# Four output stores moved from SyncE's DMA queue to ScalarE's, in a fused attention and expert-mixture kernel

## The chip, the cores and the metric

The kernel runs on one NeuronCore of a Trainium2 chip. The metric is the device time in microseconds (us) of one execution; lower is better. A core has five engines, each with its own instruction stream that runs in order: TensorE (PE in the profile; its weight loads are PEld), VectorE (DVE), ScalarE (ACT), GpSimd (POOL) and SyncE (SP). They wait for each other by semaphores. DMAs are issued from SyncE, ScalarE and GpSimd.

## The reference

```python
def _attn_ref(q, k, v, is_retrieval, n_sink, window):
    ...
    scores = scale * np.matmul(q, k.transpose(0, 1, 3, 2))
    ...
    mask = np.where(retr[0, :, 0, 0, None, None], full_mask, stream_mask)
    scores = np.where(mask[None, :, :, :], scores, -1000000000.0)
    ...
    a = a / (np.sum(a, axis=-1, keepdims=True) + 1e-09)
    return np.matmul(a, v).astype(np.float32)

def _moe_ref(x, domain_probs, w1, w2):
    ...
    p = domain_probs / (domain_probs.sum(-1, keepdims=True) + 1e-09)
    ...
    for e in range(E):
        h = np.maximum(x @ w1[e], 0.0)
        out += p[:, e:e + 1] * (h @ w2[e])
    return out.astype(np.float32)
```

Attention has 4 batches, 8 heads, 768 positions and 64 values per head. Three heads ("retrieval") see all earlier positions; the other five ("streaming") see 4 sink positions and a window of 64. The output, 3072 tokens of 512 values, goes through 4 experts of 512 to 1024 to 512, whose results are added with the token's weights `p`.

## The kernel before

Tokens are worked on in 24 tiles of 128. Attention runs over 8 pieces (batch and half, 384 positions each); three token tiles come out of each piece, transposed, as `xT`. The experts follow behind, interleaved with later attention pieces: the Python code emits a few matmuls of the expert work, then as much of the next attention piece as a plan allows. That emission is the order in which each engine runs its instructions; nothing reorders it afterwards.

The expert work has two forms. The first four token tiles are computed plainly, by `plain_steps`: tiles 0 to 2 together, then tile 3 alone. For each expert, eight groups of matmuls (L950, each group into one of four rotating PSUM banks named `pA`) make the hidden layer, a relu on ScalarE (L963) writes it to SBUF, and the matmuls of L971 make the output rows in a bank `pO`. VectorE (L983, L987) scales them by the expert's weight and adds them up in an fp32 accumulator `acc[nt]`. After the last expert the accumulator is complete and goes to memory by one DMA of 128 rows of 2 KB (L992).

The other twenty tiles go in pairs, by `pair_steps`. L1062 makes the hidden layers, again through the four `pA` banks, a relu on ScalarE (L1071) writes them, and the products of L1095 follow.

Both forms share one large SBUF buffer, `hA`. The accumulators lie in parts of it that the pairs use as blocks of hidden values:

```python
    blocks = hA.rearrange("p (b k x) -> p b k x", b=6, k=KT)
    ...
    def acc_of(nt):
        n0 = 2 * FTP * CH + nt * 2 * DM if nt < 3 else 6 * KT * P - 2 * DM
        return hA[:, n0 : n0 + 2 * DM].bitcast(FP32)
```

By these offsets `acc[0]` and `acc[1]` lie in block 3, `acc[2]` in block 4 and `acc[3]` in block 5. The third relu of the first pair writes the start of block 3, so it has to wait until the store of `acc[0]` has read it.

SyncE's queue also carries, in order of emission: the weights of a pair spread over all partitions (`pB`, L1012), the transposes of the next attention piece's queries (`qT`, three of them, L268) and keys (`kR` for retrieval heads, `kS` for streaming heads, L255), the copies of the sink rows (L249, L250), transposes of attention outputs (`xT`, L701) and the stores of the pairs (L1123). GpSimd issues the loads from memory (`kRr`, `kSr`, `q`, `vR`, `vS`). Around the end of the plain tiles SyncE's order is: `xT`, `pB`, three `qT`, `kR`, sink row, sink copy, `kS`, the four stores, and then the sink copies and transposes for the following attention piece.

The four stores are emitted at four places: three as the tiles 0, 1 and 2 end, in the last expert's turn, and the fourth as tile 3 ends. On ScalarE the exponentials of attention (L645), the relus (L963, L1071) and the row factors of streaming heads (L757, L767) run in the order of emission.

Of the kernel before, what the change touches and what calls it, by code (L numbers as in the profile page):

```python
# [17 lines left out]
def kernel(  # L18
# [33 lines left out]
    nc = tc.nc  # L52
    P = 128
# [44 lines left out]
    def bank():  # L98
        return pA.tile([P, 512], FP32, name="pA", bufs=4)
# [263 lines left out]
    for h in range(H):  # L363
        if h == 2:
            nc.sync.dma_start(
                out=v_s32, in_=v[0, :, 0:NS, :].rearrange("h r d -> r h d")
# [16 lines left out]
        out=probs, in_=moe_domain_probs.rearrange("(t p) e -> p t e", p=P)  # L383
# [121 lines left out]
    def mm_ns(cols):  # L505
        return cols / 2.4 + 2.5
# [424 lines left out]
    acc = {}  # L931
# [5 lines that stand above are left out]
    def plain_steps(nt0, tiles, e, tokens, n0):  # L937

        cols_n = tiles * P
        hs = hA[:, n0 : n0 + FTP * cols_n].rearrange("p (f x) -> p f x", f=FTP)  # L940
        require(nt0 // 3)
        x = tokens()
        ahead = 4 if nt0 == 0 and e == 0 else 1
        for f0 in [0, *range(ahead, FTP)]:
            pss = {ft: bank() for ft in range(f0, f0 + (1 if f0 else ahead))}
            cts = (0, 2, 1, 3)

            def layer1(ft, n):
                ct = cts[n]
                nc.tensor.matmul(  # L950
                    out=pss[ft][:, 0:cols_n],
                    lhsT=w1sb[:, e * DMP + ct, ft * P : (ft + 1) * P],
                    rhs=x[:, ct, :],
                    start=(n == 0),
                    stop=(n == DMP - 1),
                )

            for ft in pss:
                for n in range(DMP - 1):
                    layer1(ft, n)  # L960
            for ft, ps in pss.items():
                layer1(ft, DMP - 1)
                nc.scalar.activation(  # L963
                    out=hs[:, ft, :], in_=ps[:, 0:cols_n], func=AF.Relu
                )
                yield DMP * mm_ns(cols_n), 0.6
        for j in range(tiles):
            nt = nt0 + j
            ps_o = pO.tile([P, DM], FP32, name="pO", bufs=2)
            for ft in range(FTP):  # L970
                nc.tensor.matmul(  # L971
                    out=ps_o,
                    lhsT=hs[:, ft, j * P : (j + 1) * P],
                    rhs=w2sb[:, e * FTP + ft, :],
                    start=(ft == 0),
                    stop=(ft == FTP - 1),
                )
                if ft == FTP // 2 - 1:
                    yield FTP // 2 * mm_ns(DM), 1.4
            p_ap = p_sb[:, nt, e : e + 1]  # L980
            if e == 0:
                acc[nt] = acc_of(nt)
                nc.vector.tensor_scalar(  # L983
                    out=acc[nt], in0=ps_o, scalar1=p_ap, scalar2=None, op0=ALU.mult
                )
            else:
                nc.vector.scalar_tensor_tensor(  # L987
                    out=acc[nt], in0=ps_o, scalar=p_ap, in1=acc[nt],
                    op0=ALU.mult, op1=ALU.add,
                )  # L990
            if e == E - 1:
                nc.sync.dma_start(out=out[nt * P : (nt + 1) * P, :], in_=acc[nt])  # L992
            yield FTP // 2 * mm_ns(DM), 1.4

    PT = 2
# [170 lines left out]
    def moe_steps():  # L1166
        for e in range(E):
            if e == 1:
                turn_probs()
            yield from plain_steps(0, 3, e, lambda: xT[0], (e % 2) * FTP * CH)  # L1170
            weight_sums(e)
        for e in range(E):
            n0 = 2 * FTP * CH + 3 * 2 * DM + (e % 2) * FTP * P
            yield from plain_steps(3, 1, e, lambda: xT[1][:, :, 0:P], n0)
            if e + 1 < E:
                last_weight_sum(e)
            if e == E - 3:
                scale_inputs(pairs[0], 0)
        for n, nt0 in enumerate(pairs):
            yield from pair_steps(nt0, pairs[n + 1] if n + 1 < len(pairs) else None)  # L1180
# [56 lines left out]
    def require(a):  # L1237
        drained = False
        while state["a"] <= a:
            attention_step()  # L1240
            drained = True
        if drained:
            tick(LAG)
# [48 lines left out]
```

## Time and profile before

| | us |
|---|---|
| median of 4 runs | 398.21 (397.71 to 400.85) |
| the profiled execution | 398.11 |
| its span, first to last instruction | 396.3 |
| PE busy in the span | 378.5 (96%) |
| ACT, DVE, POOL busy | 233.9, 219.3, 139.8 |
| stores of the plain tiles, from issue to landing | 7.1 (median of 4, 256 KB each) |
| stores of the pairs, from issue to landing | 2.7 (median, 256 KB each) |

The span is what the profile's times are measured in; the execution's own time has some 1.8 us more around it. An engine that is busy 96% of the span sets the time, so the question for any edit is whether that engine's idle time changes. A wait in the profile is put down to the event that ended it: "A <- B" is time that A's engine stood before A until B was done. A busy share is an average over stages, and the stage in which the edit lies, from 70 to 110 us, is read by itself.

### The profile page before, as it was taken

What the parts mean: (1) busy time and instruction counts of PE and PEld (TensorE: products, weight loads), DVE (VectorE), ACT (ScalarE), POOL (GpSimd) and SP (SyncE); (2) the same over time, 40 slices, a digit from 0 to 9 for tenths busy, and PEclk for the clock granted to TensorE, in tenths of its full rate; (3) what the DMA queues carried; (4) which work ended last, traced back from release to release, by engine and by line L of the source; (5) the groups of instructions that cost most, each with busy time, mean ns of one, the idle gap of its engine ahead of it and who ended that gap; (6) DMA issues with size and microseconds to landing.
All of it is one profiled execution on the core that took longest, in us unless ns stands there. A gap on an engine that the chain in (4) does not pass through costs nothing.

```text
span 396.3 us, 9358 instructions
## 1 busy us (share of the span) xinstructions
PE 378.5 (96%) x3814; PEld 314.2 (79%) x3814; DVE 219.3 (55%) x472; ACT 233.9 (59%) x476; POOL 139.8 (35%) x182
## 2 busy tenths in 40 slices
PE   7889999989599998999999999999999999999996
PEld 4655556657498887889988898889988898888885
DVE  7734787556166456565653556655644547454340
ACT  4743568645468777574774578574774568361640
POOL 8833655927407533660464004651300000000000
PEclk9989999999899999999999999999999999999999
DMA  8999999999999999999899936999790210110101
GB/s 163 158 206 196 182 186 173 149 107 151 204 146 139 158 154 96 140 170 165 103 152 126 129 95 51 142 205 135 96 178 2 69 55 12 55 53 2 55 0 55
DMA packets 167632, 47.67 MB, mean 120 GB/s; under 512 B 156493, under 2 KB 161317, under 8 KB 167589
## 3 DMA queue, kind: packets, MB, share of 16 engines
q0 software_dynamic: 102656, 20.98, 69.2%
q1 hardware_dynamic: 63332, 25.70, 35.4%
q8 instruction: 30, 0.49, 0.5%
q10 hardware_dynamic: 1600, 0.39, 0.5%
q14 instruction: 14, 0.11, 0.1%
HBM read 48.82 MB, written 6.34 MB: 139 GB/s over the span
## 4 chain that ended last, share of the span: by engine, by line
PE 69%; DMA 11%; issue 8%; POOL 7%; ACT 2%; DVE 1%; POOLq 0%; ACTq 0%
PE pA L1062 28%; PE pO L1095 24%; PE pA L950 5%; PE pO L971 4%; DMA vS<-in_v_dram 3%; PE pA L627 3%; DMA kR<-kRr 3%; POOL vS L281 2%; DMA q<-in_q_dram 2%; DMA vS<-sinks 2%; PE pV L675 1%; DMA kS<-kSr 1%; PE pV L739 1%; POOL vR L279 1%; ACT es L645 1%
## 5 line engine op out<-in xcount | busy, mean ns | idle before, releaser
L1062 PE MATMUL pA<-xs,w1sb 128*128 128x256 f16 x1280 | 148.4, 274 | 4.2 <-ACT hA L1071 4.2
L1062 PEld LDWEIGHTS <-w1sb 128*128 128x128 f16 x1280 | 124.2, 98 | 19.5 <-issue 4.4
L1071 ACT ACTIVATE hA<-pA 128x512 f16<-128x512 f32 x160 | 94.8, 597 | 46.7 <-PE pA L1062 38.2
L1095 PEld LDWEIGHTS <-hA 128*128 128x128 f16 x1120 | 105.7, 98 | 12.5
L645 ACT ACTIVATE es<-pA 128x384 f16<-128x384 f32 (+2 forms) x122 | 59.9, 511 | 33.6 <-PE pA L627 30.9
L1095 PE MATMUL pO<-w2sb,hA 128*128 128x256 f16 x640 | 79.0, 272 | 0.0
L1028 DVE TENSOR_TENSOR xs<-xT,pB 128x1024 f16<-128x1024 f16 (+1 forms) x52 | 49.6, 974 | 23.5 <-PE pA L1062 23.2
L1095 PE MATMUL pO<-tsb,hA 128*128 128x256 f16 x480 | 59.8, 272 | 0.0
L281 POOL DMA_DIRECT2D vS<-in_v_dram x30 | 29.3, 985 | 81.6 <-PE pV L739 48.3
L919 DVE TENSOR_TENSOR hA<-hA 128x1024 f16<-128x1024 f16 (+1 forms) x80 | 41.4, 553 | 1.0
L233 POOL DMA_DIRECT2D kSr<-in_k_dram x30 | 29.6, 999 | 17.1 <-DMA kS<-kSr 11.5
L963 ACT ACTIVATE hA<-pA 128x384 f16<-128x384 f32 (+1 forms) x64 | 22.2, 386 | 18.6 <-PE pA L950 17.8
L649 DVE TENSOR_TENSOR es<-es,mC 128x256 f16<-128x256 f16 (+1 forms) x42 | 10.6, 257 | 39.4 <-ACT es L645 39.0
L950 PE MATMUL pA<-xT,w1sb 128*128 128x384 f16 (+1 forms) x256 | 31.6, 273 | 0.1
L971 PE MATMUL pO<-w2sb,hA 128*128 128x512 f16 x128 | 30.6, 379 | 0.0
L649 DVE TENSOR_TENSOR es<-es,mS 128x384 f16<-128x384 f16 (+1 forms) x40 | 13.7, 347 | 24.8 <-ACT es L645 24.8
L627 PE MATMUL pA<-qT,kR 128*128 128x384 f16 (+2 forms) x120 | 24.0, 278 | 2.6 <-DMA kR<-kRr 1.7
L1113 ACT COPY s<-pO 128x256 f32<-128x256 f32 x30 | 11.2, 372 | 25.5 <-PE pO L1095 23.6
L950 PEld LDWEIGHTS <-w1sb 128*128 128x128 f16 x256 | 19.3, 98 | 8.2 <-issue 0.3
L762 DVE TENSOR_TENSOR xT<-pV,rc 64x384 f16<-64x384 f32 x37 | 20.4, 554 | 9.0 <-ACT rc L767 6.8
L1036 DVE TENSOR_TENSOR hA<-hA 128x512 f16<-128x512 f16 (+1 forms) x30 | 15.3, 510 | 16.9 <-ACT hA L1071 16.7
L757 ACT ACTIVATE rc<-pV,eps 64x384 f32<-64x384 f32 x37 | 21.3, 576 | 4.4 <-PE pV L739 3.7
(113 smaller groups left out, 334.9 us busy)
## 6 DMA issues: line engine op xcount, KB each, us to landing
pB<-p_rows SPq DMA_DIRECT2D x10, 512.0 KB, 5.1
out_dram<-o SPq DMA_DIRECT2D x19, 256.0 KB, 2.7
w1sb<-in_moe_w_dram POOLq DMA_DIRECT2D x8, 512.0 KB, 10.5
w2sb<-in_moe_w_dram POOLq DMA_DIRECT2D x4, 1024.0 KB, 13.4
kSr<-in_k_dram POOLq DMA_DIRECT2D x30, 112.0 KB, 6.9
vS<-in_v_dram POOLq DMA_DIRECT2D x30, 112.0 KB, 4.2
q<-in_q_dram POOLq DMA_DIRECT2D x18, 128.0 KB, 9.7
vR<-in_v_dram POOLq DMA_DIRECT2D x24, 48.0 KB, 6.4
```

Source lines behind the costliest of these rows:

```text
L233: gp.dma_start(out=kSr[:, :, SH.index(h), own(h)], in_=windows_of(k, b, h, c),)
L281: gp.dma_start(out=t[:, :, own_v(h)], in_=windows_of(v, b, h, c))
L627: nc.tensor.matmul(out=ps[:, o : o + nq], lhsT=key_tile(b, c, h, t), rhs=qTs[b, c][:, hp, q0 : q0 + nq], start=(n == 0 or not first), stop ...
L645: nc.scalar.activation(out=es[:, 0:cols], in_=ps[:, 0:cols], func=AF.Exp, scale=SC)
L649: nc.vector.tensor_tensor(out=es[:, o0:o1], in0=es[:, o0:o1], in1=m[:, mo : mo + o1 - o0], op=ALU.mult,)
L919: nc.vector.tensor_tensor(out=out, in0=a, in1=b, op=ALU.subtract)
L950: nc.tensor.matmul(out=pss[ft][:, 0:cols_n], lhsT=w1sb[:, e * DMP + ct, ft * P : (ft + 1) * P], rhs=x[:, ct, :], start=(n == 0), stop=(n = ...
L971: nc.tensor.matmul(out=ps_o, lhsT=hs[:, ft, j * P : (j + 1) * P], rhs=w2sb[:, e * FTP + ft, :], start=(ft == 0), stop=(ft == FTP - 1),)
L1028: nc.vector.tensor_tensor(out=o, in0=xin, in1=pb.to_broadcast([P, DMP, n, P]), op=ALU.mult)
L1062: nc.tensor.matmul(out=ps[:, f * PC : (f + 1) * PC], lhsT=w1sb[:, e * DMP + ct, (f0 + f) * P : (f0 + f + 1) * P], rhs=xs[:, ct, :], start= ...
L1071: nc.scalar.activation(out=blocks[:, b0 : b0 + 2, k0 : k0 + 2, :].rearrange("p t f x -> p f t x"), in_=ps.rearrange("p (f t x) -> p f t x" ...
L1095: nc.tensor.matmul(out=ps, lhsT=a[:, k, :], rhs=b(k), start=(first and k == 0), stop=(k == KT - 1), skip_group_check=not first,)
```

## The change

The four stores of the plain tiles are issued by ScalarE instead of SyncE. Their place in the emission, their data and their size stay. In ScalarE's stream the first three stand between the last row factor of an attention piece (L767) and the relus of tile 3 (L963), the fourth between two exponentials (L645) ahead of the first pair's relus. In SyncE's stream nothing takes their place. Below the edit all lines of the changed kernel have numbers higher by one.

```diff
             if e == E - 1:
-                nc.sync.dma_start(out=out[nt * P : (nt + 1) * P, :], in_=acc[nt])
+
+                nc.scalar.dma_start(out=out[nt * P : (nt + 1) * P, :], in_=acc[nt])
             yield FTP // 2 * mm_ns(DM), 1.4
```

## The prediction

> **What bounds the kernel now.** I read the page's busy shares first: PE is busy for 378.5 of 396.3 us (96%). So only PE's idle time can be won, or made larger. Then I listed the waits between 72 and 165 us, the stretch in which the four stores stand; its columns are total us, times, longest.
>
> ```profile
> PE pA L1062 <- ACT hA L1071: 4.2, 1, 4.2
> PE pA L627 <- DMA kR<-kRr: 1.7, 1, 1.7
> ACT hA L1071 <- DMA out_dram<-hA: 5.8, 1, 5.8
> ```
>
> The third line is the cost of the stores' present place: a relu of the first pair (L1071) writes over `acc[0]`, whose store has not landed. The first line is its echo: with ACT held, no bank of `pA` comes free and PE stands. The second is a stop of its own kind, a transposed K tile that lands late. Next the timelines (start, us, what), SyncE's, then ScalarE's, then TensorE's:
>
> ```profile
> 71.38 0.46 SPq L1012 DMA_DIRECT2D pB<-p_rows  x1
> 71.94 5.60 SPq L268 DMA_TRANSPOSE qT<-q  x3
> 77.72 3.19 SPq L255 DMA_TRANSPOSE kR<-kRr  x1
> ...
> 89.67 5.89 SPq L255 DMA_TRANSPOSE kS<-kSr  x1
> 95.66 2.88 SPq L992 DMA_DIRECT2D out_dram<-hA  x4
> ```
>
> ```profile
> 73.99 0.52 ACT L767 ACTIVATE rc<-rc 64x384 f32<-64x384 f32 x1
> 77.93 1.84 ACT L963 ACTIVATE hA<-pA 128x128 f16<-128x128 f32 x8 [3.41 <-PE pA L950]
> ```
>
> ```profile
> 77.50 1.95 PE L950 MATMUL pA<-xT,w1sb 128*128 128x128 f16 x32
> 79.29 1.89 PE L971 MATMUL pO<-w2sb,hA 128*128 128x512 f16 x8
> ...
> 89.09 0.39 PE L627 MATMUL pA<-qT,kR 128*128 128x128 f16 x2 [1.74 <-DMA kR<-kRr]
> ...
> 103.55 3.55 PE L1062 MATMUL pA<-xs,w1sb 128*128 128x256 f16 x16 [4.19 <-ACT hA L1071]
> ```
>
> The first three accumulators are complete at 75.0, 76.7 and 78.45 us (DVE L987 starts at 74.25, 75.98 and 77.70, 0.75 each), yet their stores are issued at 95.66, behind `kS<-kSr`, and take 7.1 us to land. PE stands from 99.36 to 103.55. Last the stage view: length, then busy us and instructions of PE, PEld, DVE, ACT and POOL; the last three numbers are the granted clock, the DMA share and GB/s:
>
> ```profile
> 99.40:103.50 4.10, 0.00 (x0) 0.00 (x0) 0.24 (x1) 0.60 (x2) 1.23 (x2) 1.00 1.67 270
> 103.50:106.90 3.40, 3.35 (x16) 2.38 (x16) 0.23 (x1) 1.85 (x4) 3.40 (x4) 0.50 1.64 174
> ```
>
> After the stop PE runs 3.4 us at half clock: 16 matmuls of L1062 take 3.55 us there, 1.91 us at 107.13.
>
> **What the Trainium skill says.** "DMA: Bandwidth & Descriptors", section "Issuing engines are not separate DMA queues": DMAs of all engines run on the same 16 DMA engines; another issuer saves only sequencer time. The same page, "Queues, rings and completion order": SyncE and ScalarE each own one ring per DMA engine, and a DMA engine goes round the rings by packets. The trace agrees for one ring: the stores' packets begin near 100 us, after those of `kS<-kSr` (ended by 98). Its section "Anatomy of one DMA" says that a DMA's semaphore wait is kept by the issuing sequencer, so what is queued behind it waits too; SyncE's timeline fits, no run here shows it on ScalarE in mid-kernel. "TensorE: Matmul & The Clock Gate", Part 1: a free-running window of about 3.4 us of idleness halves the clock for at least another. The trace agrees: two half-clock stretches of 3.41 us, after stops of 4.19 us (above) and of 2.5 us (18.98 to 21.46), none after the 1.74 us at 87.34.
>
> **The change, part by part.**
>
> *Removed from SyncE:* four issues, 2.88 us at 95.66. Behind them stand the sink copies and transposes for the next attention; they move up by at most 2.9 us. PE first waits for none of these after 107 us by name (next `qT`, `kR`: issued by 109.2, used at 125.6), so I count nothing. If that cover were gone it would be a gain.
>
> *The late stop goes.* In the ring of ScalarE the first store no longer follows `kS<-kSr` and lands long before ACT needs it at 97.08. PE gains 4.19 us of standing and 3.55 - 1.91 = 1.64 us of half clock: **5.83 us**. What is late next there is `kS<-kSr`, landed at 101.74 by its semaphore, wanted by L627 at 106.91.
>
> *Added to ScalarE:* the built program puts stores 1 to 3 directly behind the activation that ends at 74.5, and ahead of the 24 relus of tile 3 that begin at 77.93. Each store has two waits. One is on DVE, for its accumulator. The other is on the DMA semaphore that it takes over: eight go round among the SyncE and ScalarE DMAs in program order, and a DMA waits for its semaphore's last user. For store 1 that is `xT<-x_pair` (landed 74.46), for store 2 `pB` (77.93), for store 3 the first `qT` transpose (80.52), times from the trace's semaphore records. On SyncE these had long landed. On ScalarE the third is **2.1 us later than the accumulator**.
>
> So ACT is free at 80.52 + contention + one issue. Contention: store 1 (256 KB, data from about 76) shares the engines with `pB` and `qT`. A store alone moves its data in about 0.75 us (365.8 to 373 us); I take half, 0.4, bounds 0 to 1.5. Issue: 0.52 (the four ScalarE issues of L381), bounds 0.33 (L1123) and 0.89 (longest L992). Stores 1 and 2 are issued inside the hold. Sum: 80.52 + 0.4 + 0.52 = 81.4, plus a first relu of 0.3: PE can go on at **81.7**.
>
> PE meanwhile fills four `pA` banks, 16 of the 32 matmuls of L950, by 78.46, and stands 3.2 us. By the two stops shown, that is enough for a half clock in most phases of the free-running window: another 1.64. From there PE has 87.34 - 78.46 = 8.9 us of work to the wait for `kR`, so it arrives at 90.6, or at 92.2 with half clock. Before, it waited there until 89.09.
>
> *Contention on `kR`:* 768 KB enter engines that are already shared with POOL's loads and SyncE's transposes. Three stores cost 2.2 us of all engines at most by the lone price; lower bound 0, since nothing is taken out of that stretch that could speed it; taken 1.2. `kR` then lands at 90.2, hidden behind PE's own delay.
>
> So the delay carried past `kR` is 92.2 - 89.09 = **3.1 us** with half clock, 1.5 without. `kS<-kSr` waits for a copy that landed at 89.59; it shifts by the same 1.2, to 102.9. PE arrives there at 106.91 - 5.83 + 3.1 = 104.2 (no wait) or at 102.6 (0.3 of wait).
>
> *Store 4* waits on DVE until 95.3 in its new place and on a semaphore freed at 88.8. It holds back one exponential and two relus by 94.73 to 95.8, 1.1 us. PE has four banks and needs the first of them again at 97.3: nothing. If ACT were held 1 us longer, PE would lose that excess.
>
> *Sum:* 5.83 - 3.1 = 2.7 us off. The profiled execution took 398.11 us (span 396.3), 0.1 below the median of 398.21, so the prediction is 398.2 - 2.7 = **395.5 us**. After 107 us PE is almost without stops, and POOL's loads there are released by PE itself, so the shift should be kept.
>
> **The rivals.**
>
> *B, the clock holds.* The idle 3.2 us straddle two windows. Then 5.83 - 1.5 - 0.3 = 4.0: 394.2. For it: the window's phase is free. Against: a 2.5 us stop was enough once.
>
> *C, ScalarE isn't held by the semaphores.* Then ACT waits only for the accumulators: free at 79.0, PE at 79.2, hidden by the `kR` wait. The delay is that of `kR` alone, 0.5 to 1.2, with 0.7 at `kS`: gain 3.9 to 4.7, 393.5 to 394.3. Against: the waits are in the program.
>
> *D, slower: the hold outgrows the gain.* One mechanism, the third store's wait for the first `qT` transpose, which its own predecessors delay. Break-even: PE restarts at 78.46 + 5.83 + 1.75 - 1.64 = 84.4, so `qT` would land at 83.6, 3.1 us later than before. At 7 us later: 402. For it: packets of three rings interleave, and transposes are the slow ones. Against: by then only one store of 0.75 us is in flight.
>
> *E, the gain is given back:* `kS`, or the loads that its landing releases on POOL (102.27), become the late ones: 398.2. Against: in the sum PE comes 1.3 us after `kS`; the loads had landed by 114.1, and the `kS` made from them is first used at 148.2.
>
> **How the numbers follow.** Chances: the forecast 0.38, B 0.25, C 0.17, D 0.12, E 0.08. A difference of 1%, 4.0 us, is about what a measurement of this kernel can tell; the bounds are 394.2 and 402.2. Faster: half of B and nearly all of C, 0.29. Slower: D, 0.12, which I count whole because its size is open. Within: 0.59. The range is 393.3 (C) to 399.0 (E, and D near its break-even). It leaves out the rest of D and the tail below C, under 0.2.
>
> **What would show it.** Right: the wait of L1071 on `out_dram<-hA` is gone; the relus L963 start near 81.4 instead of 77.93, with PE standing about 3 us before them; a half-clock stretch between 80 and 87; no wait of PE for `kR`, or a short one; no 4.19 us stop near 100. Wrong: L963 within 1.2 us of 77.93 (C), or the stop near 100 still there under another name (E), or ACT held past 84 (D).

## The result, and the profile after

| | before | changed |
|---|---|---|
| median (us) | 398.75 (55 runs) | 398.31 (36 runs) |
| lowest and highest | 395.91, 401.57 | 395.15, 404.09 |
| ratio to before, 95% interval | | 0.9982 [0.9965, 1.0] |

The change gains some 0.7 us (0.18%), no difference that these runs can tell from none; 2.7 us were forecast. A repetition of the changed kernel gave 0.9986 [0.9963, 1.001]. The execution that was profiled took 401.34 us, well above its kernel's median, so its lines show where time goes, not how much the change costs. (The ratios leave out executions over 1.5% above the fastest of their kernel; the medians hold all.)

The waits of the changed kernel between 72 and 165 us (total us, times, longest):

```profile
...
PE pA L627 <- DMA kS<-kSr: 7.6, 1, 7.6
ACT hA L963 <- DVE tsb L919: 5.3, 1, 5.3
```

The wait of the first pair's relu on `out_dram<-hA` is gone, as forecast, and with it the stop of PE at L1062. In its place stands the second possibility that the prediction listed under "wrong": the stop near 100 is there under another name. PE now waits for the transposed keys of the streaming heads, `kS`. TensorE's timeline (start, length, what, in brackets the idle time before it and what ended it):

```profile
76.66 1.06 PE L950 MATMUL pA<-xT,w1sb 128*128 128x128 f16 x16
79.32 1.05 PE L950 MATMUL pA<-xT,w1sb 128*128 128x128 f16 x16 [1.60 <-ACT hA L963]
...
98.19 1.91 PE L1063 MATMUL pA<-xs,w1sb 128*128 128x256 f16 x16
107.74 0.51 PE L627 MATMUL pA<-qT,kS 128*128 128x54 f16 x7 [7.63 <-DMA kS<-kSr]
```

The same stretch by stage (length, busy us and instructions of PE, PEld, DVE, ACT, POOL, then granted clock, DMA share, GB/s):

```profile
100.20:107.70 7.50, 0.00 (x0) 0.00 (x0) 0.00 (x0) 0.54 (x1) 0.00 (x0) 0.66 1.29 148
107.80:112.80 5.00, 5.00 (x34) 3.74 (x35) 2.89 (x7) 1.68 (x3) 4.58 (x5) 0.50 0.99 125
```

PE stands 7.6 us, and then works 5 us at half clock. The two stretches belong together. ScalarE's and SyncE's timelines show what came before:

```profile
74.19 4.75 ACTq L993 DMA_DIRECT2D out_dram<-hA  x3
78.99 1.70 ACT L963 ACTIVATE hA<-pA 128x128 f16<-128x128 f32 x8 [5.32 <-DVE tsb L919]
```

```profile
87.70 0.62 SPq L249 DMA_DIRECT2D sinks<-kSr  x1
88.38 0.71 SPq L250 DMA_DIRECT2D kSr<-kSr  x1
93.39 9.12 SPq L255 DMA_TRANSPOSE kS<-kSr  x1
```

The three early stores hold ScalarE until 78.94. The view names VectorE for this wait; by the trace's semaphore records the third store waits until 78.55 for the landing of the first `qT` transpose (78.53), whose semaphore it takes over. PE runs out of `pA` banks at 77.72 and stands 1.60 us (3.2 were forecast); no half clock follows. The sink row is read at 87.70 (81.15 before) and `kS` issued at 93.39 (89.67 before). Its issue takes 9.12 us (5.89 before); the fourth store is issued at 94.30, and 118 of its 128 data packets move within that issue, beside the transposes. `kS` lands some 6 us later than before (107.69, against 101.74). Not all of this is the change's doing: GpSimd's first `kSr` load was issued at 69.96, 2.5 us later than before (67.50), and ahead of the first moved store, at 74.19.

**One gate decides the span.** After the stop near 100, PE has the same work left in every profile that stops there on `kS`. The time at which PE resumes at L627, plus half of the half-clock stretch that is still to run, plus a constant gives the span (half clock by the trace's records of the granted clock):

| profile | resumes | half clock left | span | constant |
|---|---|---|---|---|
| changed | 107.74 | 5.10 | 399.5 | 289.2 |
| stores 1, 2 on ScalarE (two_again) | 102.11 | 3.03 | 392.9 | 289.3 |
| stores 1, 2, 4 (skip2) | 104.37 | 5.42 | 396.3 | 289.2 |
| store 4 alone (spare_fourth) | 105.67 | 4.02 | 397.0 | 289.3 |

All sixteen profiles with this stop give 289.2 to 289.6. So what PE loses ahead of the stop costs nothing in itself, as long as PE still comes there before `kS` lands; only how the half clock falls can differ. Before, PE resumed at L1062, at 103.55 with 3.39 us of half clock left, and the constant is 291.1. It is 1.8 us more because 16 matmuls of the pairs, 1.91 us, which the changed kernel does ahead of its stop, are still to come. So a stop at L627 is as bad as the old one when `kS` comes 1.8 us later than the first store's landing did, with as much half clock. The experiments ask what makes `kS` late.

### The profile page after: what moved, and what is told of

It is laid out like the page before. It is cut to its first block, busy times and chain, and to the rows that moved or that the text cites. A ratio compares the mean times of both kernels' runs of the same rounds, so it can differ in the third digit from the quotient of the medians.

```text
span 399.5 us, 9356 instructions
## 1 busy us (share of the span) xinstructions
PE 380.2 (95%) x3814; PEld 315.5 (79%) x3814; DVE 219.7 (55%) x472; ACT 233.7 (58%) x476; POOL 138.7 (35%) x182
## 4 chain that ended last, share of the span: by engine, by line
PE 84%; DMA 6%; ACT 4%; POOL 2%; DVE 2%; issue 1%; POOLq 0%; ACTq 0%
PE pA L1063 34%; PE pO L1096 28%; PE pA L950 7%; PE pO L971 7%; PE pA L627 4%; DMA kS<-kSr 4%; DMA vS<-in_v_dram 2%; PE pV L675 2%; PE pV L739 2%; ACT es L645 1%; ACT rc L757 1%; ACT rc L767 1%; DVE xT L762 1%; POOL vR L279 1%; PE pO L400 1%
## 5 line engine op out<-in xcount | busy, mean ns | idle before, releaser
L645 ACT ACTIVATE es<-pA 128x384 f16<-128x384 f32 (+2 forms) x122 | 59.9, 511 | 40.6 <-PE pA L627 36.7
L963 ACT ACTIVATE hA<-pA 128x384 f16<-128x384 f32 (+1 forms) x64 | 22.1, 386 | 20.4 <-PE pA L950 14.3
L950 PE MATMUL pA<-xT,w1sb 128*128 128x384 f16 (+1 forms) x256 | 31.6, 273 | 1.7 <-ACT hA L963 1.6
L649 DVE TENSOR_TENSOR es<-es,mS 128x384 f16<-128x384 f16 (+1 forms) x40 | 13.7, 347 | 32.2 <-ACT es L645 32.1
L950 PEld LDWEIGHTS <-w1sb 128*128 128x128 f16 x256 | 19.3, 98 | 9.9 <-issue 2.0
L1114 ACT COPY s<-pO 128x256 f32<-128x256 f32 x30 | 11.2, 372 | 25.1 <-PE pO L1096 23.5
L627 PE MATMUL pA<-qT,kR 128*128 128x384 f16 (+2 forms) x120 | 24.1, 279 | 0.6 <-ACT qT L538 0.4
L627 PE MATMUL pA<-qT,kS 128*128 128x55 f16 (+4 forms) x255 | 16.8, 196 | 8.2 <-DMA kS<-kSr 7.6
L1037 DVE TENSOR_TENSOR hA<-hA 128x512 f16<-128x512 f16 (+1 forms) x30 | 15.3, 510 | 16.9 <-ACT hA L1072 16.7
## 6 DMA issues: line engine op xcount, KB each, us to landing
w2sb<-in_moe_w_dram POOLq DMA_DIRECT2D x4, 1024.0 KB, 13.9
```

Source lines behind the costliest of these rows:

```text
L627: nc.tensor.matmul(out=ps[:, o : o + nq], lhsT=key_tile(b, c, h, t), rhs=qTs[b, c][:, hp, q0 : q0 + nq], start=(n == 0 or not first), stop ...
L645: nc.scalar.activation(out=es[:, 0:cols], in_=ps[:, 0:cols], func=AF.Exp, scale=SC)
L950: nc.tensor.matmul(out=pss[ft][:, 0:cols_n], lhsT=w1sb[:, e * DMP + ct, ft * P : (ft + 1) * P], rhs=x[:, ct, :], start=(n == 0), stop=(n = ...
```

## The experiments

The expectations speak of several theories. **A**: the data of the early stores slow GpSimd's `kSr` loads, and so the sink row, the copy after it and `kS`. **B**: the hold of ScalarE by the stores' waits is what costs. Later **T** (the third store costs, by its hold and its data) and **F** (the fourth costs, by its data beside `kS`'s transposes). Each ratio is against the kernel before, timed beside the run; they rest on 7 to 36 executions of a kernel.

| run | stores on ScalarE | other edit | ratio, 95% interval |
|---|---|---|---|
| again | all | none | 0.9986 [0.9963, 1.001] |
| none | no stores at all | | 0.9946 [0.9919, 0.9972] |
| rows16 | all, an eighth of the rows | | 0.9943 [0.9918, 0.9968] |
| late | all, the first three at about 85 us | | 0.9943 [0.9911, 0.9976] |
| spare | none | `acc[0]`, `acc[1]` elsewhere | 0.9911 [0.9873, 0.9949] |
| spare_act | all | `acc[0]`, `acc[1]` elsewhere | 1.0003 [0.9981, 1.0024] |
| spare_fourth | 4 | `acc[0]`, `acc[1]` elsewhere | 0.997 [0.9951, 0.999] |
| first | 1 | | 0.992 [0.9892, 0.9947] |
| first_again | 1 | | 0.9917 [0.9894, 0.9939] |
| two | 1, 2 | | 0.99 [0.9871, 0.9929] |
| two_again | 1, 2 | | 0.9904 [0.9872, 0.9936] |
| three | 1, 2, 3 | | 0.9943 [0.9923, 0.9964] |
| skip2 | 1, 2, 4 | | 0.9979 [0.9954, 1.0004] |
| third16 | all | store 3 with 16 rows | 0.9957 [0.9926, 0.9988] |
| fourth16 | all | store 4 with 16 rows | 0.9961 [0.9939, 0.9983] |
| after_order | all | `kSr` loads before `vR`'s | 0.9994 [0.9968, 1.002] |
| before_order | none | `kSr` loads before `vR`'s | 0.9991 [0.9967, 1.0015] |

**again, none, rows16, late.** The changed kernel once more, and three edits of its stores: all four left out (none, whose diff is against the kernel before), 16 of the 128 rows of each (rows16), and the first three issued in tile 3's third expert (late).

```diff
-            if e == E - 1:
-                nc.scalar.dma_start(out=out[nt * P : (nt + 1) * P, :], in_=acc[nt])
```

```diff
-                nc.scalar.dma_start(out=out[nt * P : (nt + 1) * P, :], in_=acc[nt])
+                nc.scalar.dma_start(out=out[nt * P : nt * P + 16, :], in_=acc[nt][0:16, :])
```

```diff
+        if nt0 == 3 and e == E - 2:
+            for n in range(3):
+                nc.scalar.dma_start(out=out[n * P : (n + 1) * P, :], in_=acc[n])
...
-            if e == E - 1:
+            if e == E - 1 and nt == 3:
```

> The changed kernel once more, for a second profile beside its times. Theory A (the stores' data, sent while the queries and keys of the next attention piece are on their way, delays the loads kSr, with them the sink copy and kS, so that PE stops at L627 on kS instead of at L1072): 398.3, the sink row issued at 83 us or later (81.15 before), a PE stop of 2 to 8 us on kS near 101. Theory B (ScalarE's hold for the semaphores of pB and qT gives the gain back): the relus of tile 3 start at 81 or later and PE stops 3 us or more on ACT before them, none of note on kS. Theory C (the late stop before was not worth 5.8 us in ordinary executions): no stop over 2 us in this stretch, and 398 all the same.

> The four stores of tiles 0 to 3 are left out, so those 512 rows of the output are not written. No wait of a relu for them, no hold, no data. A and B: both costs are gone, 5.83 us less the wait that is then late at kS (0.7): 393 to 394.5. C: 397.5 to 398.7.

> The four stores stay on ScalarE with the same two waits each, but carry 16 of their 128 rows, so 448 rows of the output are not written: an eighth of the data, all of the hold. A: 393.5 to 395, near the kernel without stores. B: 397.5 to 399, as the changed kernel. C: 398.

> Stores of tiles 0 to 2 on ScalarE, but issued behind the relus of tile 3's third expert (about 87 us), when their accumulators and the semaphores they take over are ready and the DMA engines run empty (share 0.05 from 88 to 90 before). All data, next to no hold, another time. A: 394 to 395.5. B: the same, so the kernel with 16 rows decides between them. C: 398.

The second profile of the changed kernel has the same form: PE stands 1.9 us at L950 and 8.2 us on `kS`. Without any store PE still stands 3.9 us on `kS` (97.76 to 101.69): `kS` stands close behind the old stop, whatever the stores do. rows16 keeps each store's place and waits and gains as much as leaving the stores out. That spoke for A, for the data, but not cleanly: ScalarE was held less too (PE stood 0.6 us at L950, not 1.6), and both gain less than A had expected: their medians, 397.6 (none) and 396.7, miss its 393 to 395. The run late is inconclusive, as its median, 399.0, and its ratio contradict each other. In its profile the stores' data fell on `kS`'s transposes, whose issue took 11.2 us.

**spare and first.** Two ways to remove the wait with little or nothing moved to ScalarE: the two accumulators in another tile (spare), or one store moved (first, first_again).

```diff
+    accs = []
...
+        if nt < 2:
+            if not accs:
+                accs.append(moe.tile([P, 2, DM], FP32, name="o", bufs=1))
+            return accs[0][:, nt, :]
```

```diff
-                nc.sync.dma_start(out=out[nt * P : (nt + 1) * P, :], in_=acc[nt])
+                eng = nc.scalar if nt == 0 else nc.sync
+                eng.dma_start(out=out[nt * P : (nt + 1) * P, :], in_=acc[nt])
```

> The kernel before, stores on SyncE behind kS as there, but acc[0] and acc[1] lie in the SBUF tile o of the pairs, which is idle until 112 us: no relu waits for a store. Theory A2 (what ends the stop near 100 us is kS, by the chain kSr loads, sink row, sink copy, transpose; the store's landing came only 1.1 us behind it in the same ring): as the kernel without stores, 395.8 to 397.0, with a PE stop of 2 to 4 us named kS at L627. Theory B2 (the relu's wait is the cost, and goes whole): 392.5 to 393.5, no stop over 1 us there.

> Only the store of acc[0], the one that the relu waits for, goes out by ScalarE; the other three stay on SyncE. No hold (its semaphore is free at 74.5), a third of the early data. A2 with the data's contention: between the changed kernel and the one without stores, 396.7 to 397.7. If the data do not matter but the wait does: 393 to 395. If neither: 398.2.

> Unchanged from the run with only the store of acc[0] on ScalarE, for a second profile and more times. Theory A: median 395 to 396, ratio 0.990 to 0.994; no stop of PE over 4 us near 100, and the sink row issued by 82.5. Rival (the gain of that run was one of the execution that was profiled and of few times): ratio above 0.996 and a stop of over 5 us on kS.

Both are faster than the kernel before by 0.8 to 0.9%, and than the changed one. This is what taking the late stop away is worth, with `kS` where it is: 3.2 to 3.5 us. (The median of spare, 395.6, lies just below the first range expected for it, that of first, 395.4, between its ranges.) One profile of first has no stop near 100, but not because `kS` came sooner: it landed at 102.80. PE came later, after a stop of 2.11 us on `kR` (to 89.15) and a half clock from 90.4 to 93.8. In the other PE stood 3.65 us on `kS`, with the sink row read at 86.81 (81.08 in the first), against the expectation of 82.5. How late the sink row is thus varies from execution to execution, while the times agree.

**after_order, before_order.** If late `kSr` loads were the cause, issuing them ahead of three `vR` loads should help:

```diff
+        load_k(b, c, SH)
         load_v(b, c, RH)
-        load_k(b, c, SH)
```

> The changed kernel with the loads kSr issued ahead of the loads vR on GpSimd, so some 2.3 us earlier. A2: kS lands 2 us earlier, 396.0 to 396.8. Rival (kS is late because its own transposes run slowly beside the other queues, whenever they begin): 398.0 to 398.6, kS lands no earlier than 107.

> The kernel before with the same reorder of GpSimd's loads. A2: kS and the stores behind it in SyncE's queue move up, 396.3 to 397.3. Rival (the transposes' own pace): 397.9 to 398.5.

Neither moved the time. In the profile of after_order the sink row is read at 85.00, 2.7 us earlier than in the changed kernel's, yet `kS` lands at 107.15, only 0.5 us earlier. That of before_order has `kS` 3.1 us earlier than before, but it is the fastest of its 22 executions. So an earlier start of these loads buys nothing that can be measured, and A lost its main support.

**spare_act, two, two_again, before_again.** The price of the move alone, the dose, and a second profile of before. In spare_act the edit of spare is joined by the first of these, two has the second alone:

```diff
-                nc.sync.dma_start(out=out[nt * P : (nt + 1) * P, :], in_=acc[nt])
+                nc.scalar.dma_start(out=out[nt * P : (nt + 1) * P, :], in_=acc[nt])
```

```diff
-                nc.sync.dma_start(out=out[nt * P : (nt + 1) * P, :], in_=acc[nt])
+                eng = nc.scalar if nt < 2 else nc.sync
+                eng.dma_start(out=out[nt * P : (nt + 1) * P, :], in_=acc[nt])
```

> acc[0] and acc[1] lie in a tile of their own, so that no relu waits for a store, and all four stores go out by ScalarE as in the changed kernel: against the run with the accumulators moved alone (395.59) this is the price of the early stores by itself, with the stop that they were to remove gone in both. Theory A (the early data of three stores slow POOL's kSr loads and through the sink row make kS late): 397.5 to 398.6, as the changed kernel, ratio about 0.998, with PE standing 5 to 8 us at L627 on kS near 100. Rival (the early stores cost nothing; the changed kernel loses its gain to something else in acc[0]'s and acc[1]'s old place): 395.0 to 396.2, ratio about 0.991.

> The stores of acc[0] and acc[1] go out by ScalarE, those of acc[2] and acc[3] by SyncE: 512 KB early instead of 256 (395.38) or 768 (398.3). Theory A with a cost in proportion to the early data: 396.4 to 397.4, ratio about 0.995. Rival (it is the third store alone that costs, by its semaphore's wait for the first qT transpose or by landing on the kSr loads): 395.0 to 396.0, ratio about 0.992.

> Unchanged from the run with the stores of acc[0] and acc[1] on ScalarE and the two others on SyncE, for more times and a second profile. If the two early stores cost nothing that shows: 394.3 to 395.8, ratio 0.988 to 0.993. Rival (each early store costs its part and the first measurement had few times): 396 to 397.4, ratio 0.993 to 0.997.

> The kernel before unchanged, for a second profile. Theory A: the sink row issued within 1.5 us of 81.15, kS issued within 1.5 us of 89.67, and PE's stop near 100 again at L1062, on the store of acc[0], 3 to 5 us. Rival (how late kS comes varies from execution to execution as much as the early stores move it): sink row after 83.5 or kS issued after 92 without any early store.

With the wait gone by placement in both, spare_act and spare differ by the move alone: it costs 0.9%, the whole gain. But it isn't a cost in proportion to the early data: two stores cost nothing that shows (0.990 and 0.990, on 8 and 7 executions; the median of two_again, 396.14, lies in the rival's range). The traces do show the effect of A: from the first `kSr` load's issue to the sink row 11.8 to 13.7 us pass in the six profiles without full early stores (before, before_again, none, rows16, spare, spare_fourth) and 15.4 to 18.0 in eight with two or three of them (three itself, at 14.3, apart; 13.9 and 15.3 with one). It just doesn't decide the time up to two stores. The second profile of before has its stop at L1062 again, 6.9 us (3 to 5 expected), with `kS` issued at 90.72.

**three, skip2, third16, fourth16, spare_fourth.** These ask which of the last two stores costs. The first line is that of three, against two; the condition is `nt != 2` in skip2, and `nt == 3`, together with the edit of spare, in spare_fourth. The other diff is third16, against the changed kernel; fourth16 has `nt == 3`.

```diff
-                eng = nc.scalar if nt < 2 else nc.sync
+                eng = nc.scalar if nt < 3 else nc.sync
```

```diff
-                nc.scalar.dma_start(out=out[nt * P : (nt + 1) * P, :], in_=acc[nt])
+                n_ = 16 if nt == 2 else P
+                nc.scalar.dma_start(out=out[nt * P : nt * P + n_, :], in_=acc[nt][0:n_, :])
```

> The first three stores go out by ScalarE, the fourth (acc[3]) by SyncE as before. Two early stores had cost nothing (394.63, ratio 0.990), all four cost the whole gain (398.3, ratio 0.998). Theory F (the fourth store costs: its data go out during kS's transposes, whose issue took 9.1 to 9.5 us in the profiles with it and 5.9 to 7.6 in most without): 394.5 to 396, ratio 0.989 to 0.993, kS's issue 6 to 8 us. Theory T (the third store costs, by its hold of ScalarE and by its data on the kSr loads): 397.5 to 398.6, ratio 0.996 to 1.000. If both cost: 396 to 397.5.

> Stores 1, 2 and 4 (acc[0], acc[1], acc[3]) go out by ScalarE, the third (acc[2]) by SyncE. Theory F (the fourth costs): 397.5 to 398.6, ratio 0.996 to 1.000, kS's issue over 8.5 us, relus of tile 3 starting at 77 to 78. Theory T (the third costs): 394.5 to 396, ratio 0.989 to 0.993. If both cost: 396 to 397.5.

> The changed kernel, but the store of acc[2] carries 16 of its 128 rows (112 rows of the output stay unwritten); its place, its waits and so its hold of ScalarE stay. Theory F: no change from the changed kernel, 397.5 to 398.6, ratio 0.996 to 1.000. Theory T by data: 394.5 to 396, ratio 0.989 to 0.993, sink row within 15.5 us of the first kSr load. Theory T by the hold alone: as F, so the run is read together with the two others.

> The changed kernel, but the store of acc[3] carries 16 of its 128 rows (112 rows of the output stay unwritten); its place and waits stay. Theory F by data: 394.5 to 396, ratio 0.989 to 0.993, kS's issue below 8 us. Theory F by the store's hold of ScalarE at 95: no change, 397.5 to 398.6. Theory T: no change, 397.5 to 398.6, kS late by its sink row.

> acc[0] and acc[1] lie in a tile of their own (no relu of the first pair waits for their stores) and only the fourth store, that of acc[3], goes out by ScalarE; the others stay on SyncE. Against the same placement with all stores on SyncE (395.59, ratio 0.991) this is the price of the fourth store's move alone. Theory F+T (the fourth costs about 0.4% by its data beside kS's transposes, the third the other 0.4%): 396.5 to 398, ratio 0.994 to 0.998, kS's issue over 8.5 us, sink row within 14 us of the first kSr load. Rival (the fourth costs only together with the three early stores): 395 to 396.2, ratio 0.989 to 0.993, kS's issue below 8 us.

The fourth costs in each comparison: added to three it takes the ratio from 0.9943 to 0.9982, added to two from 0.990 to 0.9979, and alone, against spare, from 0.9911 to 0.997. The third costs when it is added to two (0.990 to 0.9943), but nothing when the fourth is on ScalarE already (0.9979 to 0.9982), and skip2 came out as F alone had expected. The intervals, some 0.2 to 0.3% each way, don't tell whether the two costs add up.

**The fourth store** is best seen in two profiles that agree up to its issue. SyncE in two_again, then in skip2:

```profile
85.63 0.61 SPq L249 DMA_DIRECT2D sinks<-kSr  x1
...
91.89 7.06 SPq L255 DMA_TRANSPOSE kS<-kSr  x1
```

```profile
85.63 0.62 SPq L249 DMA_DIRECT2D sinks<-kSr  x1
...
91.59 10.08 SPq L255 DMA_TRANSPOSE kS<-kSr  x1
```

The sink row is read at the same time and `kS` issued 0.3 us earlier in skip2, yet its issue takes 3.0 us longer. The DMA queues of the two between 96 and 100 us show what moved meanwhile (packets, MB, share of the time of 16 DMA engines; q1 is SyncE's ring, q0 GpSimd's, q10 ScalarE's):

```profile
q1 hardware_dynamic: 2697, 0.69, 110.5%
q0 software_dynamic: 667, 0.08, 40.9%
```

```profile
q1 hardware_dynamic: 1536, 0.39, 98.9%
q0 software_dynamic: 324, 0.04, 18.4%
q10 hardware_dynamic: 80, 0.15, 17.2%
```

The transposes' ring moves 1536 packets in place of 2697, although the store takes only 80 packets. PE pays for it at L627, again two_again first:

```profile
102.11 0.51 PE L627 MATMUL pA<-qT,kS 128*128 128x54 f16 x7 [3.78 <-DMA kS<-kSr]
```

```profile
104.37 0.51 PE L627 MATMUL pA<-qT,kS 128*128 128x54 f16 x7 [6.71 <-DMA kS<-kSr]
```

It resumes 2.3 us later, and the spans are 392.9 and 396.3. In spare_fourth, with no early store, SyncE's timeline shows a long issue too:

```profile
90.93 9.84 SPq L255 DMA_TRANSPOSE kS<-kSr  x1
```

But there the store's data move from 99.23 on, half of them after the issue has ended. And the issue is short in two profiles with a full fourth store (third16, 6.67; after_order, 7.32), and long in one without (spare, 8.86). So its length doesn't measure the store's cost; the way to the landing is nearer to it. In all eight profiles with a full fourth store on ScalarE its 128 packets moved before `kS` landed. From `kS`'s issue to PE's going on, 9.2 to 12.1 us pass in seven profiles that stop there without a full fourth store on ScalarE, and 11.9 to 16.9 in eight that have it. One profile goes against this: three, 15.0 us without it, in an execution of 402.0 us, the longest of its runs. fourth16, whose fourth store keeps its place and waits, shows the traces' side (9.9 us), but its time, 0.9961, missed the 0.989 to 0.993 expected by F, and its interval overlaps the changed kernel's. So the times show that the fourth store's move costs; that it costs by its data is what the matched pair and most profiles show, and no time shows it by itself.

**The third store** holds ScalarE. In third16 it carries an eighth of the data, and here the view names the DMA:

```profile
ACT hA L963 <- DMA qT<-q: 6.3, 1, 6.3
...
PE pA L950 <- ACT hA L963: 2.6, 1, 2.6
```

The relus stand behind the third store, which waits for the landing of the first `qT` transpose (79.56). PE stands 2.6 us and then runs at half clock:

```profile
80.35 1.86 PE L950 MATMUL pA<-xT,w1sb 128*128 128x128 f16 x16 [2.58 <-ACT hA L963]
```

16 matmuls of L950 take 1.86 us there and 1.05 in the changed kernel's line above. In two, two_again and skip2, without the third store, PE doesn't stand at L950 at all, and ScalarE's relus wait only for PE. The hold is shown; that it is the third store's cost is not. In all eight profiles with the third store at its early place on ScalarE, PE stands 0.6 to 2.6 us at L950, and later 2.0 to 8.2 us on `kS`, in each of them for longer. By the gate above PE would without the hold only have stood longer on `kS`, and `kS`'s own way, from the `kSr` loads over the sink row and the copy, doesn't pass through ScalarE. The times don't settle it either. rows16 (the hold with little data) and three (with all data) both stand at 0.9943, but so does none, at 0.9946, with neither; and third16's ratio has a wide interval that its median, 399.38, contradicts. How the third store costs stays open.

It also stays open why none, without any store, isn't as fast as two. Leaving four DMAs out also shifts the order in which the later ones take over semaphores; that wasn't tried by itself.

## Why the prediction was wrong

- *The late stop goes, 5.83 us.* The mechanism was right: the wait of L1071 is gone. Its size was not. `kS` stands close behind the old stop, and PE meets it with another half clock. In the runs that pay nothing for the move the gain is 3.2 to 4.0 us (0.8 to 1.0% of 398.5).
- ***Store 4: nothing.* This step failed.** It was judged by what it holds back on ScalarE, and PE indeed doesn't stand for that. Its data were not counted: 256 KB run beside the transposes of `kS`, the very transfer that the prediction had named as the next to be late. Measured: 0.4 to 0.8%, 1.6 to 3.1 us.
- ***`kS` shifts by the same 1.2 us, to 102.9; no wait.* This step failed with it, and it decides the result.** `kS` landed at 107.69 in the changed kernel's profile and PE stood 7.6 us. The contention was booked for the early stores on `kR`, which landed at 87.80 and stopped nobody; the path from `kSr` loads over the sink row to `kS` was followed only by that shift.
- *The hold by the third store's semaphore.* Right in kind, and too large: ScalarE was free at 78.94, not 81.4, as the first `qT` landed at 78.53 and not at 80.52 plus contention. PE stood 1.6 us, without half clock; in third16 it was 2.6 us with it. The 3.1 us booked for it assume that PE comes to L627 after `kS`. PE came at 100.11 and stood until 107.74, so by the gate above the hold itself cost nothing there. What the third store was measured to cost, 0.1 to 1.6 us by what it is added to, isn't explained by it. The stop for `kR` is gone, as forecast.
- *The half clock.* The prediction calls the trace in agreement with the window of idleness that it cites, but its own second stop, 2.5 us, is shorter than that window. What the profiles show instead stands at the end.
- *Rivals.* B and C need no late `kS`, and fell. C's sign, the first relu within 1.2 us of 77.93, did appear (78.99), although ScalarE was held: the stage ran 0.84 us earlier in this execution (the last row factor at 73.15, 73.99 before). So the sign didn't tell the two apart. D fell: the hold never reached its break-even. E, "the gain is given back", happened, by its first branch, and had a chance of 0.08. The argument against it, that PE comes 1.3 us after `kS`, came from one profile of before, as if `kS`'s landing were fixed.

The sum by the runs, in one order: 3.9 us gained (two), 1.6 given back when the third store is added, 1.6 when the fourth is: 0.7 left, the measured 0.18%. In the other order (two, skip2, all) the fourth takes 3.1 and the third 0.1; the runs don't fix the split. Two of the prediction's errors cancel in part: the gain and the hold were both booked too high.

The Trainium skill's sentence in "DMA: Bandwidth & Descriptors", section "Issuing engines are not separate DMA queues", that another issuer saves only the sequencer's time, which is usually small, holds here only when the waits ahead in the issuer's stream are counted in: the first store was issued at 74.19 us in place of 95.66, and from there took as long to land as before (7.2 us, against 7.1). The page's section "Queues, rings and completion order", by which a DMA engine serves the rings in turn, fits what the move did to the neighbour: in SyncE's ring the stores' packets came after those of `kS` (from 99.8 us on, before), in ScalarE's the fourth store's came among them (96.2 to 103.1).

## What to carry to other kernels

When a store is moved out of a queue, ask of each single transfer what will be moving at its new time: the one that PE needs next should have the DMA engines. Move only what somebody waits for: two of the four stores on ScalarE give 0.990 of the time before, all four 0.998. Before booking a stop as a gain, find the landing that stands next behind it, and how much that varies over two or three profiles of the same kernel.

## What was not expected of the hardware

- A store on another ring can come with a large loss for DMA transposes: in one matched pair of profiles, with 80 of its packets (2 KB each) in 4 us, the transposes' packets (256 bytes: 0.69 MB in 2697) fell to 1536.
- A stop is paid twice: 3.78 us of standing was followed by 3.0 us at half clock, 7.63 us by 5.1, and 2.58 us by 3.2. But 1.60 us was followed by none. In the twenty profiles, from 26 us to PE's last work, each of the 21 stops of PE of 2.01 us or more brought a half clock, none of the 9 from 1.40 to 1.90 us did, and there was no half clock without such a stop.
- A DMA's semaphore, taken over from an earlier DMA, can hold a compute engine that issues it: in third16, 6.3 us of ScalarE's time ended with the landing of `qT`, which none of its relus reads.
